# A new order and new PSUM homes for the first 552 steps of a retention and PReLU kernel on one core

## The chip, the cores and the metric

The kernel runs on one core of a Trainium2 chip. The metric is the device time of one execution in microseconds (us). A core has five engines that each work through their own queue in order: TensorE (PE; its weight loads are listed apart as PEld), VectorE (DVE), ScalarE (ACT), GpSimd (POOL), and SyncE (SP), which here issues nearly all DMA transfers. SBUF is the on-chip memory; PSUM holds matmul results in eight banks.

## The reference

```python
# q, k, v: (8, 8, 576, 64) float32
scores = scale * np.matmul(q, k.transpose(0, 1, 3, 2))
gamma = 1.0 - 2.0 ** (-5.0 - np.arange(H))
Dmat = np.where(rel >= 0, gamma[:, None, None] ** rel[None], 0.0)   # rel = i - j
attn = np.matmul(scores * Dmat, v)                                  # retention, per head
x = attn.transpose(0, 2, 1, 3).reshape(B * S, H * D)                # (4608, 512)
h = x @ w_in                                                        # w_in: (512, 2048)
g = np.maximum(h, 0.0) + alpha * np.minimum(h, 0.0)                 # alpha: (2048,)
out = g @ w_out                                                     # w_out: (2048, 512)
```

Both weights come as 64-bit floats; the kernel makes 32-bit ones of them on the chip.

## The kernel before, in words

**Retention.** A sequence of 576 positions is cut into nine chunks of 64. Within a chunk the masked product of q and k is formed; from chunk to chunk a running state (the sums of k times v, decayed) is carried. The first two batches are done in six "parts" of four, four and one chunks (all heads at once); the other batches later in pairs of heads ("joints"). For a part, SP loads the natural rows of k, q and v (`load_part`, into rooms of the tiles called w, so that the profile says `w<-in_k_dram`), GpSimd scales q and v by tables of powers of gamma (L351), TensorE transposes k and q (L375; L535 for the one-chunk part) and ScalarE copies the transposes out (L381, L538). Then come the products of q and k (L399) and VectorE's mask (L406), the states k times v (L422) with VectorE's sums (L435, L437), and the output, first from the masked scores (L470), then from the states (L493). Between L470 and L493 ScalarE makes a copy of one element (L482, "spy") that L493 waits for. ScalarE copies the result to the x tiles (L514). The one-chunk part has L548, L561 and L568 for these products.

A joint loads q and k in a form that VectorE can transpose (qx, kx; L722 in all), scales qx on GpSimd (L716), scales a natural k on ScalarE (kn, at L725 to L727), and forms scores and states on TensorE (L796, L803, L806), then the masks (L824), the carried sums (su, L836 to L847), and two copies by DMA into the tiles that the next joint's values product reads (L744): qT into `at`, su into `vn`.

**Weights.** A quarter of a weight unit is loaded as 64-bit words and turned into 32-bit floats by a chain: ScalarE (L613, L615), VectorE (L623, L625, L634), GpSimd (L637). After the first eight cells (see below), weights and activations are split into three parts each, so that fast 32-bit rounded matmuls add up to full precision: ScalarE L666, GpSimd L668 and VectorE L670 for weights, and the like for x and g.

**The MLP.** Tokens go in 18 blocks of 256, hidden columns in eight units of 256. The first eight (block, unit) cells use plain 32-bit matmuls, since their split weights don't exist yet: L974 for `x @ w_in`, ScalarE L980 and VectorE L985 for the PReLU, L1005 for the second product. All later cells use the split form (L1071, L1105 and L1223, L1167 at the end). While these run, the joints of the later batches are woven in between.

**Fills.** At the start there are matmuls whose result nobody reads: `burn` (L1297, 64 by 64 tiles with 16 columns, six groups of eight) and `fill` (L1288, 128 by 128, 15 in all). They are steps like others and have places in the order.

**What sets the order.** The kernel does not emit instructions as it is written. Every step is recorded by `do(engine, cost, function, reads, writes)`; 3811 steps are recorded. At the end the list ORDER, written out as numbers of steps, is gone through from its start, and each step then emits its instructions. So ORDER sets the order of every engine's queue, SP's among them; semaphores follow from the reads and writes. In the same way, each time a step needs a new PSUM tile, `Gen` takes the next digit of the string BANKS as its bank:

```python
if slot and slot.bank:
    slot = banks[int(next(banked))]
...
for now[0], n in enumerate(order):
    op = ops[n]
    ins = op.fn()
```

SP's loads are held back, too: for the first LIMITED entries of ORDER, `dma` makes a load wait for an earlier one's landing, so that no more than 1 MB (up to entry 130) or 1.25 MB is in flight:

```python
if now[0] < LIMITED:
    ahead = size
    for other, n in reversed(flight):
        if eng == "SP" and ahead >= (IN_FLIGHT if now[0] >= FRONT else IN_FRONT):
            tc.add_manual_dep(...)      # wait until `other` has landed
            break
        ahead += n
```

All loads by SP are recorded at L224 in the profile.

Of the kernel before, what the change touches and what calls it, by code (L numbers as in the profile page):

```python
# [21 lines left out]
def kernel(  # L22
# [126 lines left out]
    for i in range(2):  # L149
# [6 lines left out]
        "200535545661702405070423172047436234654317545707176141645461704500066171106600717116602607"  # L156
        "060167247052344635472107161067706117062653241061707601706104253461761006176107255234700761"
# [80 lines left out]
    LIMITED, IN_FLIGHT = 486, 5 << 18  # L238
# [1316 lines left out]
    for i, (va, vb) in enumerate(two):  # L1555
# [30 lines left out]
        "68-70 67 3 71 1-2 0 4-5 53 24 66 12 25 86 9 13-14 33 16 10 15 22 7 17 80 23 19 8 85 32 47 18 21 20 "  # L1586
        "27 48-50 84 6 115 83 51 26 64 55 52 28-29 56-57 87 81 118 58 119 88 30 59 62 82 63 40 114 116 65 60 "
        "154 112 34 31 54 117 110 113 11 72 111 36-37 139 61 136 138 140 38 142 35 153 141 137 171 41 43-44 "
        "89 39 42 168 143 94 166 144 95 103 73 145 90 45 146 46 155 147 181 156-157 209 182 75 170 183 76-77 "
        "102 158 74 159 91 93 160 92 212 161 184 162-163 204 78 121-122 97 176 185 129 96 98 177 99 104 100 "  # L1590
        "173 205 124 106 164 105 120 208 169 337 101 188-189 130 107-109 213 123 132 172 196 125-126 148 210 "
        "149 127 167 133 150 246 197 131 211 229 206-207 152 134-135 330 230 151 190 192-194 217 216 218 178 "
        "180 186 247 179 257 219 244 198 128 270 220 250 221 331 199 245 187 332 175 191 200 271 201-202 174 "
        "222 454 223 234-235 203 224-227 333 195 284-285 231 236 293 259 336 272 456 237 451 238-239 232-233 "
        "292 228 274 258 453 455 248 275 273 260-261 252 262 251 445 276 243 253 452 249 214 254 242 255 240 "
        "263 241 277 286 349 447 266 288 268 289-290 267 269 215 372 256 294 296-298 287 291 303 302 306 342 "
        "374 304 295 305 282 466 307 281 338 334 299 278 436 279 264 350 265 280 446 340 343 315 352-353 339 "
        "335 345 354 351 448 439 316 344 346 358 365 317 553 384 347 355 348 320 366 321 318-319 373 308 475 "
        "322 375 341 433 309 437 385 301 399 435 442 552 300 377 398 310-312 323-324 328 313 378 434 325 443 "
        "283 379 383 327 329 314 367 369 368 440 438 356 450 382 457 376 460 381 326 397 441 380 462 404 461 "  # L1600
        "79 415 414 360 467 413 361 405-410 402 458 411 400 412 417 419 359 362 416 363 423 422 421 165 364 "
        "403 401 444 392 463 393 386 459 387 468 357 465 481 555 482 420 424 449 388 418 394 426 464 396 425 "
        "472 490 370 473 395 522 488 519 523 483 520 526 489 495 529 487 507 469 496 389 497-498 390 499 524 "
        "501 505 427 506 478 504 517 500 503 539 493 485 568 371 502 428 492 484 521 530 527 476 528 534-535 "
        "540 532 541 516 508 533 430 391 542 491 536 543 537 544 494 545 470 538 582 486 514 474 480 581 509 "
        "583 477 510 512 511 513 515 431 471 618 595 584 531 588 570 590 596 546 597-599 569 586 563 548 585 "
        "594 547 593 571 549 564 607 587 479 601 604 600 561 589 616 562 565 620 572 566-567 573-575 606 554 "
        "592 634 603 619 605 636 602 577 591 432 635 617 614 551 608 576 615 610 550 637 578 621 638-639 "
        "622-623 640 651 609 612 655 624 652 429 648 641 653 611 613 658-661 654 662 674 579 643 665-668 656 "
        "697 647 669 663 670 695 671 696 664 688 672-673 690 675 689 580 677 687 657 649 642 644 698 645 650 "  # L1610
        "699-701 691-694 686 721 684 676 702 704 720 679 678 722 685 730 518 723 703 758 705 734-735 680-681 "
        "646 726 683 729 682 711 761 727 762 733 717 706 759 728 724 746 763 707-708 716 736 712 781 731 737 "
        "744 754 772 760 738-740 783 713-714 756 718 709 774-775 784 743 732 741 755 742 782 556 773 745 747 "
        "785-786 525 751 719 779 776 787 710 752-753 777 725 780 748 778 840 749-750 715 794-796 793 807 841 "
        "805 802 789 788 790 798 797 842 803 808-809 800 817 791 804 833 799 810 834 811-812 814 831 813 816 "
        "820 832 843 806 819 815 852 818 801 835 854 828-829 853 830 792 855-856 918 915 557 838 821 827 857 "
        "916 824 836 858 822 837 877 859 823 919 880 826 878 861 920 879 860 885 887 881 891 886 892-893 825 "
        "894 839 895 889 901 864 897 873 896 869 900 899 888 862 868 870-871 898 917 903 883 902 875 863 930 "
        "932 884 931 882 874 890 923 933 558-559 912 921 934 865-866 924 904 935 914 922 910 928 913 936 905 "
        "907 925 943 911 872 944 906 908 945-946 926-927 999 955 952 929 967 957 953 966 958-959 956 909 937 "  # L1620
        "954 876 948 960-962 939 942 969 949 951 991 1002 938 940 947 979 950 963 965 1004 968 998 1000 1003 "
        "1005-1007 992 964 867 757 971 989-990 993 1008 994 997 978 560 970 976 995 941 1028 625 1027 974 "
        "1029 1038 1001 977 1009 973 1010 975 1011 1050 1037 1041 1030 1068 1012 996 1065 1013 1042 1069 1014 "
        "1066 1015 1018 1067 1019 1051 1016 1071 1036 1035 972 1043-1044 1072 1020 1070 1073 1053 1034 1045 "
        "1047 1024 1046 1089 1033 1074-1075 1040 1049 1091 1048 1090 1063 1076 1052 1021 1079 1077 1092 1032 "
        "1055 1093 1039 1094 1060 1054 1064 1061 1095 1023 1017 1025-1026 1062 1031 1078 1059 1102 1056 1103 "
        "1111 1105 1104 1112 1141 1097 1110 1116 1106 1096 1098 1115 1099 1107 1100 1058 1113 1125 1148 1139 "
        "1057 1127 1117-1120 1122 1109 1121 1142 1114 1140 1126 1154 1150 1128 1152 1108 1153 1155 1143-1145 "
        "1124 1123 626 1101 1156 1129 1157 1371 1130 1022 1158 1147 1137 1159 1179 1136 1160-1161 628 1138 "
        "1177 1218 1178 1187 1162 1146 1163 1180 1149 1132 1219 1135 1133 1215 1220 1165 1201 1188 1164 1190 "  # L1630
        "1238 1131 1134 1185 1191 1216-1217 1192-1194 1239 1195 1197 1196 1203 1200 1173 1168 1175 1186 1240 "
        "1183 1231 1198 1166 1202 1170 1212 1184 627 1169 1151 1211 1174 1241-1242 1205 1232 1229 1204 1176 "
        "1199 1230 1171 1237 1243 1233 1181 1236 1244 1214 1208 1234 1206 1182 1235 1245-1246 1189 1210 1207 "
        "629-630 1253 1265-1266 631 1267 1252 1268-1269 1251 1261 1271 1247 1209 1213 1254 1249 1275 1288 "
        "1264 1289 1255 1298 1263 1270 1248 1274 1260 1262 1259 1277 1290-1292 1276 1295 1258 1257 1273 1279 "
        "632 1285-1286 1272 1293-1294 1278 1167 1287 1311 1297 1299 1172 1309-1310 1250 1312 1256 1313 1372 "
        "1314 1282 1315 1281 1336 1375-1376 1316 1284 1318 1335 1317 1334 1346 1348 1280 1349 1338 1357 1319 "
        "1350 1296 1331 1326 1345 1351 1330 1325 1283 1320 1373 1344 1352-1353 1342 1322 1446 1337 1377 1327 "
        "1341 1321 1374 1354 1358 1343 1328 633 1387 1355 1360 1378 1388 1379 1356 1389 1359 1340 1362 764 "
        "1369 1332 1300 1347 1339 1361 1390 1370 1323 1364 1391 1380 1366 1381-1382 1392-1393 1363 1383 1401 "  # L1640
        "1400 1402 1333 1413 1384 1447 1365 1367-1368 1404 1324 1411 1405 1412 1409-1410 1386 1459 1456 "
        "1414-1415 1455 1416-1417 1408 1407 1385 1423 1425 765 1418 1420 1419 1457 1424 1421 1403 1395 1406 "
        "1394 1460 1396 1422 1426 766 1427 1397 1461-1463 1436 1448 1521-1522 1449 1398 1430 1399 1434 1523 "
        "1453 1464 1450 1465 1485 1428 1524 767 1329 1435 768 1432-1433 1431 1484 1492 1451-1452 1466 1468 "
        "1467 1469 1491 1486 1498-1499 1493 1500 1454 1476 1501-1503 1429 1487 769 1508 1525 1480 1507 1528 "
        "1526 1489 1527 1496 1470 1495 1472 1490 1481 1504 1494 1471 1473 1546 770 1475 1547 1477 1505-1506 "
# [161 lines left out]
```

## Time and profile before

| | us |
|---|---|
| median of 3 runs | 915.4 (915.34 to 915.81) |
| profiled execution, its own time | 915.47 |
| its span in the profile | 913.4 |
| TensorE busy in it | 906.3 |
| granted TensorE clock (share of full) | 0.999 |

The profile is one execution on the core. "Busy" is the time in which an engine has an instruction running; matmuls are pipelined and their ends are modelled, so that short waits of TensorE can hide in busy time. A wait is put down to the engine or DMA that released it last. The view of waits gives total us, times and the longest; the timeline gives start, duration, engine, line, operation, output and inputs, with the idle time before it in brackets; the windows give busy us of each engine in a stretch, the clock, the mean busy share of the 16 DMA engines (which can read slightly over 1) and GB/s.

### The profile page before, as it was taken

How to read it: one execution, taken by the hardware profiler on the slowest of the kernel's cores; microseconds unless marked ns; L12 is line 12 of the kernel's file. 1: busy time of each engine (PE TensorE's matmuls, PEld its weight loads, DVE VectorE, ACT ScalarE, POOL GpSimd, SP SyncE). 2: the span in 40 equal slices, each digit the busy share in tenths (PEclk: the TensorE clock that was granted, in tenths of full speed). 3: DMA queues.
4: the chain of work that ended last, by engine and by line, in shares of the span. 5: the costliest groups of instructions: out<-in, count | busy, mean ns of one | idle time of the engine just before them, and what ended most of it. 6: DMA issues, size and time to landing. Idle time of an engine off the chain costs nothing. (4 is left out here: it accounts for less than half of the span.)

```text
span 913.4 us, 19163 instructions
## 1 busy us (share of the span) xinstructions
PE 906.3 (99%) x7331; PEld 739.6 (81%) x7331; DVE 549.6 (60%) x1004; ACT 500.7 (55%) x1011; POOL 520.3 (57%) x461
## 2 busy tenths in 40 slices
PE   9999999999999999999999999999999999999998
PEld 8767788887788888888888888888888888888886
DVE  5797767757768776576756776434444534444243
ACT  4575665556555665666746565636363636364441
POOL 4587665556556665756542335666655657574624
PEclk9999999999999999999999999999999999999999
DMA  9999778788898888775243332212122222211112
GB/s 204 245 232 185 172 173 184 166 204 186 185 200 192 205 208 189 177 182 167 70 141 130 99 115 82 70 58 81 57 93 64 91 82 76 93 47 47 46 47 70
DMA packets 235948, 121.34 MB, mean 133 GB/s; under 512 B 203456, under 2 KB 203728, under 8 KB 235856
## 3 DMA queue, kind: packets, MB, share of 16 engines
q1 hardware_dynamic: 235712, 119.98, 52.3%
q8 instruction: 58, 0.95, 0.5%
q14 instruction: 34, 0.28, 0.1%
q10 hardware_dynamic: 144, 0.13, 0.0%
HBM read 74.19 MB, written 32.51 MB: 117 GB/s over the span
## 5 line engine op out<-in xcount | busy, mean ns | idle before, releaser
L1223 PE MATMUL pso<-w,g 128*128 128x512 f32 x1344 | 330.3, 392 | 0.0
L1223 PEld LDWEIGHTS pso<-w,g 128*128 128x128 f32 x1344 | 249.9, 188 | 54.3 <-POOL g L1150 1.6
L1147 POOL TENSOR_TENSOR g<-ga_all,g 128x512 fp32r<-128x512 f32 x76 | 98.2, 1295 | 131.5 <-ACT g L1143 101.8
L1150 POOL TENSOR_TENSOR g<-g 128x512 fp32r<-128x512 f32 x114 | 147.3, 1295 | 19.4 <-DVE su L949 5.7
L1071 PE MATMUL psa<-lx_x,w 128*128 128x512 f32 (+1 forms) x288 | 70.3, 377 | 0.2 <-DVE at L824 0.2
L1071 PE MATMUL psh<-lx_x,w 128*128 128x512 f32 (+1 forms) x272 | 68.2, 384 | 0.1
L1143 ACT ACTIVATE g<-ga_all 128x512 fp32r<-128x512 f32 x76 | 47.8, 631 | 36.6 <-PE pso L1223 17.5
L1139 POOL TENSOR_TENSOR g<-g 128x512 fp32r<-128x512 f32 x22 | 28.5, 1297 | 61.8 <-DVE g L1136 34.4
L1071 PEld LDWEIGHTS psa<-lx_x,w 128*128 128x128 f32 x288 | 51.4, 188 | 12.1 <-issue 1.3
L1071 PEld LDWEIGHTS psh<-lx_x,w 128*128 128x128 f32 x272 | 49.6, 188 | 11.2 <-issue 0.6
L1223 PE MATMUL pso<-lx_x,g 128*128 128x512 f32 x216 | 53.5, 390 | 0.1
L1147 POOL TENSOR_TENSOR g<-vn,g 128x512 fp32r<-128x512 f32 x25 | 32.4, 1297 | 37.2 <-ACT g L1143 34.5
L1145 ACT ACTIVATE g<-ga_all 128x512 fp32r<-128x512 f32 x76 | 47.2, 624 | 5.8 <-PE pso L1223 4.0
L1046 POOL TENSOR_TENSOR lx_x<-lx_x 128x512 fp32r<-128x512 f32 x28 | 35.9, 1293 | 23.1 <-DVE lx_x L1043 18.9
L1223 PEld LDWEIGHTS pso<-lx_x,g 128*128 128x128 f32 x216 | 40.4, 188 | 9.0 <-DVE o L1246 0.6
L1241 DVE TENSOR_TENSOR op<-pso,op 128x512 f32<-128x512 f32 x35 | 24.0, 686 | 31.2 <-PE pso L1223 31.2
L1071 PE MATMUL pso<-lx_x,w 128*128 128x512 f32 (+1 forms) x160 | 37.8, 370 | 0.0
L1105 PE MATMUL psh<-w,w 128*128 128x512 f32 x144 | 34.6, 389 | 0.0
L1105 PE MATMUL psa<-w,w 128*128 128x512 f32 x144 | 34.6, 389 | 0.0
L716 POOL TENSOR_TENSOR qx<-qx,tabx 128x576 f32<-128x576 f32 x24 | 27.6, 1149 | 9.6 <-DMA qx<-in_q_dram 5.9
L1071 PEld LDWEIGHTS pso<-lx_x,w 128*128 128x128 f32 x160 | 28.0, 188 | 5.7 <-ACT o L1245 0.6
L1147 POOL TENSOR_TENSOR g<-x,g 128x512 fp32r<-128x512 f32 x13 | 16.9, 1298 | 26.2 <-ACT g L1143 24.7
(408 smaller groups left out, 1968.2 us busy)
## 6 DMA issues: line engine op xcount, KB each, us to landing
xk<-x SPq DMA_DIRECT2D x18, 512.0 KB, 3.7
ok<-o SPq DMA_DIRECT2D x36, 256.0 KB, 2.7
op<-ok SPq DMA_DIRECT2D x18, 512.0 KB, 4.0
out_dram<-o SPq DMA_DIRECT2D x35, 256.0 KB, 2.3
x<-xk SPq DMA_DIRECT2D x16, 512.0 KB, 5.5
kx<-in_k_dram SPq DMA_DIRECT2D x96, 72.0 KB, 3.3
qx<-in_q_dram SPq DMA_DIRECT2D x96, 72.0 KB, 3.3
kn<-in_k_dram SPq DMA_DIRECT2D x48, 144.0 KB, 3.6
```

What stands on the lines that cost most here:

```text
L716: return nc.gpsimd.tensor_tensor(out=qh, in0=qh, in1=tabx[:, None, c, :, None].to_broadcast([P, NJ, 2, 32]), op=ALU.mult)
L1046: do("POOL", 1.29, lambda h=h, l=l, d=d: nc.gpsimd.tensor_tensor(out=piece(d()), in0=h(), in1=l(), op=ALU.subtract), [(g, 0, n), (g, 1, n) ...
L1071: nc.tensor.matmul(out_of(p), w[:, c0:c0 + P], xp(l, cc), start=(l != 1 and cc == 0), stop=(l > 0 and cc == NCC - 1))
L1105: nc.tensor.matmul(p.get(), w[:, c0:c0 + P], piece(words_of(g)[:, o:o + DM]), start=(l != 1 and cc == 0), stop=(l > 0 and cc == NCC - 1))
L1139: do("POOL", 1.29, lambda: nc.gpsimd.tensor_tensor(out=piece(to.get()[:, 2]), in0=to.get()[:, 0], in1=to.get()[:, 1], op=ALU.subtract), [( ...
L1143: do("ACT", 0.64, lambda: nc.scalar.mul(piece(to.get()[:, 2]), whole(), BELOW), both, [(to, 2)])
L1145: do("ACT", 0.64, lambda: nc.scalar.mul(piece(to.get()[:, 0]), whole(), BELOW * 2.0 ** -12), both, [(to, 0)])
L1147: do("POOL", 1.29, lambda: nc.gpsimd.tensor_tensor(out=piece(to.get()[:, 1]), in0=whole(), in1=to.get()[:, 2], op=ALU.subtract), both + [( ...
L1150: do("POOL", 1.29, lambda: nc.gpsimd.tensor_tensor(out=piece(to.get()[:, 2]), in0=to.get()[:, 0], in1=to.get()[:, 1], op=ALU.subtract), [( ...
L1223: nc.tensor.matmul(a[2 * m + b].get(), piece(g.get()[:, l, f, m * P:(m + 1) * P]), w_piece(u, 2 + f, l), start=(cell["first"] and f == 0 a ...
L1241: do("DVE", 0.69, lambda: nc.vector.tensor_tensor(out=t(), in0=p1.get(), in1=t(), op=ALU.subtract), [(p1, 0)], [tk])
```

## The change

The first 552 entries of ORDER are rearranged; they are the same steps. From entry 552 on the list is unchanged. Of the first 111 digits of BANKS 77 differ, and LIMITED goes from 486 to 492. The new list and digits were found by a search in which every instruction fetch has a random time. Nothing else differs. The diff, cut to its start:

```diff
     BANKS = (
-        "200535545661702405070423172047436234654317545707176141645461704500066171106600717116602607"
-        "060167247052344635472107161067706117062653241061707601706104253461761006176107255234700761"
+        "440236123203724560764414054717561230515671214535401603745574765057165171016600717616062006"
+        "701760203652344625743107161067706117062653241061707601706104253461761006176107255234700761"
 ...
-    LIMITED, IN_FLIGHT = 486, 5 << 18
+    LIMITED, IN_FLIGHT = 492, 5 << 18
 ...
     ORDER = (
-        "68-70 67 3 71 1-2 0 4-5 53 24 66 12 25 86 9 13-14 33 16 10 15 22 7 17 80 23 19 8 85 32 47 18 21 20 "
-        "27 48-50 84 6 115 83 51 26 64 55 52 28-29 56-57 87 81 118 58 119 88 30 59 62 82 63 40 114 116 65 60 "
+        "66-67 2 68 71 3 13 1 0 4-5 69 80 53 70 9-10 85 16 12 24 17 14 25 22 83 15 7 23 86 19 8 47 18 21 84 "
+        "48 27 49 20 81 50-51 82 6 114 116 87 32 115 26 55 117 56 52 33 110 88 57-60 72 136 118-119 65 112 64 "
 ...
```

Some of the queues before and after (fill and L-numbers as above, step numbers in brackets):

```text
SP, first 21 loads (k, q, v: attention; wi, wo: w_in, w_out; al: alpha)
 before: k q q k v v | wi wi q wi al q wi k k v v wo q wo k
 after:  q k q k v v | al q wi wi k q k v wi wi v wo q wo k
PE, after the first part's states (L422)
 before: fill fill L470 L470 al L375 L493 L493 fill L375 fill L375 L375 fill L399 L399 L422 L974 L422 L974 L535
 after:  al fill L375 L470 L470 L375 L493 L493 L375 fill L375 fill fill fill L399 L399 L422 L422 L974 L974 L535
ACT, at entry 360 or so
 before: L666(475) spy(322) kn(375) L666(433) L666(442) L514 ...
 after:  L615(344) L666(433) kn(375) spy(322) L514 L514 L514 L514 ...
SP, second half of the first joint's kn (step 339)
 before: entry 332, ahead of both loads into op
 after:  entry 357, behind loads of qx, kx, both loads into op and the copy of qT into at
```

## The prediction

> **What bounds the kernel now.** I read the busy times first, then the windows, then every wait of TensorE, and last the queues around the waits in the part that the change touches.
>
> ```profile
> PE 906.3 (99%) x7331; PEld 739.6 (81%) x7331; DVE 549.6 (60%) x1004; ACT 500.7 (55%) x1011; POOL 520.3 (57%) x461
> ```
>
> TensorE is the bound: it is idle for 913.4 - 906.3 = 7.1 us. The windows (PE, PEld, DVE, ACT, POOL busy, clock, DMA share, GB/s) say where:
>
> ```profile
> 0.00:30.00 30.00, 27.57 (x609) 24.82 (x613) 20.07 (x66) 12.59 (x21) 16.08 (x29) 1.00 0.99 212
> 30.00:70.00 40.00, 40.00 (x580) 28.89 (x573) 32.13 (x56) 26.90 (x51) 27.34 (x25) 1.00 0.96 238
> 70.00:115.00 45.00, 44.67 (x678) 32.98 (x677) 35.49 (x73) 25.37 (x58) 31.59 (x28) 1.00 0.88 177
> 115.00:900.00 785.00, 784.53 (x5438) 645.38 (x5437) 457.14 (x804) 435.24 (x881) 442.67 (x380) 1.00 0.47 123
> ```
>
> The first 30 us lose 2.4, the next 85 us 0.3, the 785 us after that 0.5, and the rest is the tail. Up to 70 us the DMA engines are as full as TensorE (share 0.99 and 0.96): two bounds run side by side. The whole run's waits of TensorE (us in total, times, longest):
>
> ```profile
> PE psh L1297 <- DVE warm L101: 1.1, 1, 1.1
> PE psa L535 <- DMA w<-in_k_dram: 0.4, 1, 0.4
> PE pso L422 <- POOL w L351: 0.4, 1, 0.4
> PE psa L470 <- ACT ga_all L980: 0.3, 1, 0.3
> PE psa L375 <- DMA w<-in_k_dram: 0.2, 1, 0.2
> PE pso L1167 <- POOL g L1139: 0.2, 1, 0.2
> PE psa L1071 <- DVE at L824: 0.2, 1, 0.2
> ```
>
> All but the sixth lie ahead of 103 us, which is the stretch that is reordered. The first is the start itself.
>
> **What the change moves.** The first 552 entries of ORDER hold the same 552 steps in both kernels, and from there on the two lists are equal: by the order view that stretch ends on TensorE about 113 us in. No step is added or dropped, also not the fills and burns (L1288, L1297), which cost TensorE the same wherever they stand. So the sum has only waits in it, and switches between small and full tiles. It is made against the profiled execution: span 913.4, time 915.47, that is 2.1 outside the span and 0.07 above the median of 915.4.
>
> *Early waits.* Open to a gain ahead of 30 us: 0.4 + 0.4 + 0.2 = 1.0, and some 0.5 that the modelled ends hide (L1288 ends at 20.44 + 0.83 = 21.27, L399 starts at 21.43; others are like it). There is one alternation less: before, small L422 stands between two L974 groups, 25.50 - 23.57 = 1.93 apart, where unbroken L974 takes 41.35 - 39.63 = 1.72 for as many: 0.2. Ceiling 1.7. But then comes the wait on the load:
>
> ```profile
> 28.48 0.71 PE L535 MATMUL psa<-ident,w 64*128 64x64 f32 x8 [0.37 <-DMA w<-in_k_dram]
> ```
>
> That k load is the 21st on SP's queue in both orders, behind the same 20 loads, in a window with a DMA share of 0.99. Whatever TensorE saves ahead of it is waited away, unless the queue itself runs faster. Also, the second L422 group now stands directly behind the first, and needs GpSimd's second scaling of v:
>
> ```profile
> 21.85 2.04 POOL L351 TENSOR_TENSOR w<-w,tp 128x512 f32<-128x512 f32 x2 [2.16 <-DMA w<-in_v_dram]
> ```
>
> It ends at 23.9, and its load again has the same set ahead of it, so a new wait of about 1 us stands there, paid for out of what was saved before. From 23.9: L422 0.5, two L974 groups 3.5, switches 0.4, gives 28.3, just ahead of 28.48. Bounds for the early part: 1.7 gained to 1.0 lost; I take 0.1 gained, by the k load's row.
>
> *Middle waits.* L470's 0.3 and L1071's 0.2 can go (vector steps of L985 come sooner, another PSUM bank is written). Bounds 0 and 0.5; I take 0.3.
>
> *One dangerous place, at 80 us.* ScalarE's one-element copy L482 ("spy") releases L493, and before it stands ahead of the scaling of kn (the profile calls it L727):
>
> ```profile
> 76.53 0.13 ACT L482 COPY spy<-psh 1x2 f32<-1x2 f32 x1
> 76.57 0.77 ACT L727 ACTIVATE kn<-kn,tabk 128x576 f32<-128x576 f32 x1
> 80.32 0.27 PE L493 MATMUL psa<-w,w 64*64 64x64 f32 x2
> ```
>
> After it, L727 stands first and the spy right behind. L727 needs both halves of kn, and the second half has moved far back on SP: behind more qx and kx loads, both weight halves into op and the copy of qT. Behind the waiting L727 are queued on ScalarE the spy and four L514 copies; behind L493 on TensorE, everything. L493 is due at about 80.9 (L548, 0.56, goes ahead of it now). From kn's landing it needs 0.1 + 0.77 + 0.15 + 0.1 = 1.1, so kn must land by 79.8. When does it? Counting bytes along SP's list, the load of before with as many ahead of it is issued here:
>
> ```profile
> 76.82 0.46 SPq L224 DMA_DIRECT2D qx<-in_q_dram  x1
> ```
>
> With 4.0 to 5.2 to landing (the DMA issues from 60 to 100 us: kn 4.0, op 5.2) kn lands at 80.8 to 82.0 and L493 waits 1.0 to 2.2. Against it stands that in before SP itself stood still ahead of a weight load, held by the bound on bytes in flight:
>
> ```profile
> SPq L224 <- DMA kx<-in_k_dram: 3.3, 2, 3.2
> ```
>
> With fewer loads ahead of that weight load, up to 3.2 of this may come back, and kn lands at 77.6, with no wait. Bounds 0 and 2.2; with the DMA engines at 0.96 most of the 3.2 was not idle time, so I take 80.6, that is 0.8 lost.
>
> *Edits at no cost.* LIMITED's rise from 486 to 492 by itself reaches no load: SP's entries around it stand at 481 and 496 of the new order. PSUM homes cost nothing by themselves: a new home is a new wait on its last reader, and I found none later than those above. The su copies into vn (L224) leave about 3 us later, since six more vector steps (L722 twice, L824 four times, 3.5 us by their rows) now stand ahead of L847; the second was issued at about 88.6 and landed 2.8 later, at 91.4, and L744 reads it at 95.53, so about 1 us of cover is left; if it is gone, L744 waits by as much as it is short.
>
> Sum: 915.4 - 0.1 - 0.3 + 0.8 = 915.8.
>
> **A rule that speaks against the change.** Of the instruction fetch the page's part on DMA queues shows (packets, MB, share):
>
> ```profile
> q8 instruction: 58, 0.95, 0.5%
> ```
>
> No row of TensorE's waits names it, so here a fetch can only act through the DMA engines that it shares with loads. The Trainium skill, "Runtime: NRT & Kernel Launch", section "Instruction fetch mechanics", says that the fetch runs ahead by itself and is mostly hidden. By that rule there is nothing random to plan for, and the time would be 915.4. The trace agrees as far as TensorE's waits go; what a fetch does to a load's landing no view shows.
>
> **Rivals.**
>
> 1. *Robust front, faster.* SP's queue really runs ahead (k and v of the second part arrive sooner since two w_in loads stand behind them, the 3.2 us hold is gone), so that the early 1.7 and the middle 0.5 both come back and kn is in time: 915.4 - 2.2 = 913.2. For it: the waits are there to be had. Against it: equal sets of loads ahead of both early gates at a share of 0.99.
> 2. *The spy waits, slower.* kn lands at its late bound, 82.0, nothing later gives it back, since TensorE runs without gaps from 81 us on, and the early part loses a little: 915.4 + 2.2 - 0.3 + 0.4 = 917.7, up to 918.5 when the su copies are short as well. It decides at kn's landing: 79.8 costs nothing, and from there each us costs one; it is slower by over 0.2% beyond about 82.
> 3. *Nothing happens*, because every gain runs into the DMA queue and kn is just in time: 915.4. It lies inside the forecast's case.
>
> **How the numbers follow.** A measurement of this kernel can tell about 0.2%, 1.8 us, from no change. Forecast and rival 3 together 0.48, with a range of their own of 914.2 to 917.0; rival 1 0.17; rival 2 0.35, more than rival 1 since a gain needs several waits to go at once and a loss only one. Faster by over 0.2% (under 913.6) is rival 1, slower (over 917.2) is rival 2. The range reaches into both, to 913.2 and 918.3, and leaves out about a tenth on each side at most.
>
> **What would show it.** In the profile of the changed kernel: L535 near 28.5 still released by a DMA, or the early part was misjudged; a wait of the second L422 on POOL L351 near 23; L470 and L1071 gone from TensorE's waits; L493 near 81 with a wait on ACT L482, and ScalarE's L727 ahead of it released by kn's DMA. If L727 starts before 79.9, the 0.8 is wrong; if TensorE idles by over 1 us anywhere from 30 to 115 us at another line, so is the picture. Past 115 us every line should cost what it costs now.

## The result and the profile after

The changed kernel takes 919.74 us (median of 6, 918.91 to 921.28) beside 915.5 for the kernel before: ratio 1.005, 95% interval 1.004 to 1.0061. It is slower by 4.2 us. In three later sets of executions, each with the kernel before beside it, the same kernel stood at 1.0028 (1.0018 to 1.0038), 1.0043 (1.0031 to 1.0056) and 1.0038 (1.0025 to 1.0052): always slower, by 2.3 to 4.2 us. Why its four medians lie 2.2 us apart (917.55 to 919.74), and those of the kernel before only 0.5 (915.0 to 915.5), is part of the story. The profiled execution took 919.4 us, span 917.7.

The windows of the changed kernel (columns as before):

```profile
0.00:30.00 30.00, 26.33 (x546) 24.12 (x546) 18.35 (x64) 11.79 (x20) 14.41 (x27) 1.00 0.96 204
30.00:70.00 40.00, 39.55 (x627) 29.20 (x627) 31.19 (x55) 28.09 (x53) 27.43 (x25) 1.00 0.96 241
70.00:115.00 45.00, 43.21 (x655) 30.25 (x655) 34.75 (x67) 23.31 (x50) 28.27 (x25) 1.00 0.76 164
115.00:900.00 785.00, 784.52 (x5449) 645.96 (x5447) 457.52 (x808) 436.98 (x887) 444.73 (x382) 1.00 0.48 123
```

TensorE's idle time grows in all three early stretches: from 2.43 to 3.67, from 0 to 0.45 and from 0.33 to 1.79 us. In the last line TensorE's busy time is the same to 0.01. TensorE's waits say which ones they are (us in total, times, longest):

```profile
PE pso L535 <- DMA w<-in_k_dram: 1.6, 1, 1.6
PE psa L493 <- ACT spy L482: 1.4, 1, 1.4
PE psa L1297 <- DVE warm L101: 1.1, 1, 1.1
PE psa L422 <- POOL w L351: 0.8, 1, 0.8
PE psh L974 <- DVE su L847: 0.3, 1, 0.3
PE pso L1005 <- DVE lx_w L634: 0.3, 1, 0.3
PE psa L1071 <- DVE at L824: 0.2, 1, 0.2
```

L535's wait has grown from 0.4 to 1.6. L493's for the spy is new, so are those of L974 and L1005. L470's is gone. The timeline at the two large ones:

```profile
29.84 0.68 PE L535 MATMUL pso<-ident,w 64*128 64x64 f32 x8 [1.59 <-DMA w<-in_k_dram]
...
83.65 0.78 ACT L727 ACTIVATE kn<-kn,tabk 128x576 f32<-128x576 f32 x1 [4.73 <-DMA kn<-in_k_dram]
84.33 0.13 ACT L482 COPY spy<-psh 1x2 f32<-1x2 f32 x1
84.52 0.27 PE L493 MATMUL psa<-w,w 64*64 64x64 f32 x2 [1.44 <-ACT spy L482]
```

ScalarE stands 4.73 us in front of the kn scaling with the spy queued behind it, and TensorE stands behind the spy. kn landed at 83.63, not at 80.6.

Where the 4.2 us arise can be read from TensorE's progress: L535 starts 1.36 later than before (29.84 against 28.48), the first L1005 1.3 later (33.98 against 32.67), the second L535 group 2.3 later (75.95 against 73.65) and the first L744 4.2 later (99.76 against 95.53). At each of the last three points TensorE has done as many products in both kernels (703, 1191 and 1527). Up to L744 its idle time has grown by 3.2 us, from 2.73 to 5.91; the other 1.0 stands in no row of waits. From that L744 to the end of the span it is 817.9 us in both kernels, and 817.8 to 818.6 in all 17 profiles of this study. So the time is settled by 100 us, and a run is read by when it reaches L744:

| kernel | ratio to before (95%) | L535 | kn landed | L493 | L744 |
|---|---|---|---|---|---|
| before | 1 | 28.5 | 75.8 | 80.3 | 95.5 |
| changed, first profile | 1.0050 (1.0040 to 1.0061) | 29.8 | 83.6 | 84.5 | 99.8 |
| c_after | 1.0028 (1.0018 to 1.0038) | 28.8 | 81.7 | 82.6 | 97.9 |
| c2_after | 1.0043 (1.0031 to 1.0056) | 28.8 | 83.5 | 84.4 | 99.6 |
| c3_after | 1.0038 (1.0025 to 1.0052) | 30.4 | 84.0 | 84.9 | 100.2 |
| e1_spy_first | 1.0025 (1.0012 to 1.0039) | 28.5 | 82.8 | 81.9 | 97.2 |
| e2_k_ahead | 1.0035 (1.0023 to 1.0047) | 27.5 | 81.7 | 82.6 | 97.8 |
| e3_su_first | 1.0029 (1.0013 to 1.0045) | 28.6 | 82.1 | 83.0 | 97.7 |
| e4_burn_homes | 1.0040 (1.0027 to 1.0053) | 28.2 | 81.0 | 81.9 | 97.2 |
| e5_three | 1.0006 (0.9998 to 1.0015) | 28.6 | 80.5 | 80.6 | 95.4 |
| e7_no_spy | 1.0030 (1.0019 to 1.0042) | 29.8 | 82.7 | 83.6 | 98.3 |
| g1_both_waits | 1.0019 (1.0010 to 1.0028) | 27.3 | 81.1 | 81.3 | 96.1 |
| k1_load_early | 1.0018 (1.0010 to 1.0027) | 28.6 | 77.0 | 81.4 | 96.6 |
| e6_half_burns | 1.0049 (1.0036 to 1.0062) | 30.3 | 85.6 | 86.4 | 101.7 |
| f1_before_late | 1.0038 (1.0025 to 1.0051) | 28.4 | 82.0 | 82.9 | 99.7 |
| f3_load_only | 1.0008 (0.9999 to 1.0017) | 27.7 | 80.4 | 79.2 | 95.1 |
| h1_k_ahead | 1.0005 (0.9996 to 1.0014) | 28.0 | 75.4 | 80.0 | 95.2 |

The times of a column are those of one profile each; the ratio is over all executions of a set. The runs were made in four later sets, each with the kernel before beside it and each on another chip: e1 to e4; c_after, e5, e6 and f1; c2_after, e7, g1 and f3; c3_after, k1 and h1. From one set to another, ratios are compared.

### The profile page after: what moved, and what is told of

Its sections match the earlier page's. It is cut to its first block, busy times and chain, and to the rows that moved or that the text cites. A ratio compares the mean times of both kernels' runs of the same rounds, so it can differ in the third digit from the quotient of the medians.

```text
span 917.7 us, 19153 instructions
## 1 busy us (share of the span) xinstructions
PE 907.3 (99%) x7331; PEld 740.1 (81%) x7331; DVE 549.8 (60%) x1004; ACT 501.9 (55%) x1011; POOL 520.0 (57%) x461
## 5 line engine op out<-in xcount | busy, mean ns | idle before, releaser
L1071 PE MATMUL psa<-lx_x,w 128*128 128x512 f32 (+1 forms) x284 | 69.2, 376 | 0.2 <-DVE at L824 0.2
L1071 PE MATMUL psh<-lx_x,w 128*128 128x512 f32 (+1 forms) x272 | 68.5, 385 | 0.1
L1139 POOL TENSOR_TENSOR g<-g 128x512 fp32r<-128x512 f32 x22 | 28.5, 1295 | 61.8 <-DVE g L1136 34.4
L1071 PEld LDWEIGHTS psa<-lx_x,w 128*128 128x128 f32 x284 | 50.8, 188 | 11.5 <-issue 0.8
L1071 PEld LDWEIGHTS psh<-lx_x,w 128*128 128x128 f32 x272 | 49.6, 188 | 11.7 <-issue 1.1
L1071 PE MATMUL pso<-lx_x,w 128*128 128x512 f32 (+1 forms) x164 | 38.6, 370 | 0.1
L1071 PEld LDWEIGHTS pso<-lx_x,w 128*128 128x128 f32 x164 | 28.5, 188 | 6.5 <-ACT o L1245 0.6
L824 DVE SCALAR_TENSOR_TENSOR at<-psa,pf,mask 64x512 f32<-64x512 f32 (+1 forms) x46 | 24.0, 526 | 14.4 <-PE psa L803 6.9
L716 POOL TENSOR_TENSOR qx<-qx,tabx 128x576 f32<-128x576 f32 x24 | 27.7, 1154 | 7.3 <-DMA qx<-in_q_dram 6.0
```

Of the source, the lines that this page charges most:

```text
L716: return nc.gpsimd.tensor_tensor(out=qh, in0=qh, in1=tabx[:, None, c, :, None].to_broadcast([P, NJ, 2, 32]), op=ALU.mult)
L824: nc.vector.scalar_tensor_tensor(out=mt.get()[half(1 - h2), h2, j], in0=fro[x], scalar=pf[x, 1, h:h + 1], in1=mask[x, None, :].to_broadcas ...
L1071: nc.tensor.matmul(out_of(p), w[:, c0:c0 + P], xp(l, cc), start=(l != 1 and cc == 0), stop=(l > 0 and cc == NCC - 1))
L1139: do("POOL", 1.29, lambda: nc.gpsimd.tensor_tensor(out=piece(to.get()[:, 2]), in0=to.get()[:, 0], in1=to.get()[:, 1], op=ALU.subtract), [( ...
```

## The experiments

All edits are moves in ORDER, written as the list of step numbers, unless it says otherwise.

**The spy behind kn.** Theory: kn's second half lands late, and through the spy this holds up TensorE. Rivals: the value part L493 is late for its own inputs, or the delay is covered later. First the changed kernel with the two ScalarE steps in the old order (e1_spy_first):

```diff
-375 322 383
+322 375 383
```

> The changed kernel with one step moved: the spy copy (L482, step 322) is issued ahead of the kn scaling (L727, step 375) on ScalarE; all else stays. Theory A (kn's late landing reaches TensorE only through the queue place of the spy): the 1.4 us wait of L493 for the spy goes, L493 starts at about 83.0 instead of 84.5 us, everything behind it is 1.2 to 1.5 us earlier, and the kernel takes about 918.3 us. kn is landed at 83.6, scaled by 84.4, and its first reader (the score products L796) comes at 86.1 to 86.3, so no new wait. Rival B (the value part is late for another reason, its own inputs or its PSUM homes): L493 starts at 84.4 or later as before and the time stays at 919.7. Rival C (the score products inherit the wait for kn): less than 0.5 us comes back. Since the steps up to 80 us are the same ones, the places of the instruction packets on the DMA engines (one at 79.7 us in the changed kernel) should be seen again within 0.3 us if they follow TensorE's instruction count; if they are random, kn lands at another time.

kn landed late again, at 82.8, and TensorE did not care. ScalarE's timeline in this run:

```profile
77.90 0.13 ACT L482 COPY spy<-psh 1x2 f32<-1x2 f32 x1
82.81 0.78 ACT L727 ACTIVATE kn<-kn,tabk 128x576 f32<-128x576 f32 x1 [4.77 <-DMA kn<-in_k_dram]
```

The spy is done 4.8 us before kn is there, L493 has no wait, and it starts at 81.9. That is theory A in the profile. The instruction packet expected at 79.7 came at 78.95, with TensorE 0.9 us ahead of the changed kernel's first profile (the second L535 group at 75.05 against 75.95). In time the run (1.0025) can't be told from the unchanged kernel's 1.0028 to 1.0050, so the price needed stronger contrasts. One is the kernel before with the pair alone made late (f1_before_late), and with the load late but the spy in front (f3_load_only):

```diff
 f1, in the kernel before
-339 ... 322 375 ... 377 ... 323
+377 339 375 322 ... 323
 f3, in the kernel before
-339 ... 322 375 ... 377 ... 323
+322 ... 377 339 375 ... 323
```

> The kernel before with one part of the change alone: SyncE's kn load (339) is issued behind the qx load (377), four places later than its place before, and the spy copy (322) and the kn scaling (375) on ScalarE go behind it in the changed kernel's order (scaling first). Theory A (this pair is the largest single cause): kn lands at 82.3 to 83.5 us instead of 75.8, L727 and the spy end 0.9 us later, L493 starts at 83.4 to 84.4 us instead of 80.3, and nothing later makes up for it: 3.0 to 4.0 us slower than the kernel before, about 918.7. Rival B (the late value part is covered by what follows, since the changed kernel loses its time elsewhere): less than 1 us slower. Rival C (the load lands early although it is issued late, for lack of a fetch packet in its way): kn lands at 81.0, 1.5 to 2.2 us slower.

> f1_before_late without its second half: in the kernel before, the kn load (339) and its scaling (375) go four places later, but the spy copy (322) keeps its place ahead of the scaling. Theory A (the late kn reaches TensorE through the spy, and without that only through what ScalarE has queued behind the scaling): L493 starts at 80.1 to 80.5 us as in the kernel before, the copies L514 behind the scaling are 1.5 to 2.0 us late, the score products L796 start at 84.3 to 85.5 instead of 83.8, and the time is 0.5 to 1.7 us above the kernel before, 915.8 to 917.0. Rival B (the score products inherit the whole of it): 3.0 us or more above, as f1_before_late's 3.4.

TensorE's longest wait in f1:

```profile
PE psa L493 <- ACT spy L482: 2.9, 1, 2.9
```

f1 is 3.4 us slower than the kernel before (918.69 against 915.29), as expected; kn landed at 82.0 and L493 started at 82.9, both a little under their ranges. Not all of it is the wait. The windows of f1 around the wait (columns as before):

```profile
79.93:83.34 3.41, 0.50 (x25) 0.40 (x28) 0.00 (x0) 0.81 (x2) 1.91 (x3) 1.00 1.19 153
83.34:86.76 3.42, 3.42 (x71) 2.79 (x63) 1.23 (x3) 1.99 (x5) 0.00 (x0) 0.50 0.75 166
```

TensorE was busy for 0.50 of 3.41 us and was then granted half its clock for the next 3.42; from L493 to L744 it took 16.77 us, against 15.20 in the kernel before. Four of f1's five executions have a mean granted clock of 0.998 or less (this profile: 0.997), and none of f3's eleven has.

f3, with kn landing 4.6 us later than in the kernel before, stands at 1.0008, and its interval holds no change. L493 has no wait there, but the L514 copies queued behind the scaling now hold up another step:

```profile
PE psh L974 <- ACT x L514: 0.6, 1, 0.6
```

By the ratios, 0.0030 of 915, or 2.7 us, hang on the queue place of a one-element copy, the half clock included; the two intervals together allow 1.3 to 4.2. L493 (79.2) and L796 (82.7) started earlier in f3 than expected because L535's load landed early in that profile, at 27.45.

The other contrast moves the load instead and leaves the spy behind (k1_load_early, beside c3_after):

```diff
-553 398 552 377 339 (on SyncE)
+339 553 398 552 377
```

> The changed kernel with kn's load (step 339) issued on SyncE ahead of the 256 KB load 553 (at about 75 us) instead of four issues later behind the qx load 377 (77.5 us); ScalarE keeps the scaling ahead of the spy. Theory A (kn is late first for its place in SyncE's queue, and its last sixteenth for the instruction packet that is fetched at about 79 us, which at the earlier place is behind it): kn's fifteenth part lands at 77.6 to 78.8 us and its sixteenth within 0.5 us of it, L727 starts as soon as ScalarE is free at 78.9, the spy ends by 80.0, L493 does not wait, and the time is 0.8 to 2.2 us below the unchanged changed kernel. Rival B (the place of the spy is what counts, not the load's): L493 still waits over 0.5 us and the time is that of the changed kernel. Rival C (what is issued behind kn is now late instead: the qx load 377 or the load 552): a new wait of over 0.5 us at L796 or L1005 and less than 0.5 us gained.

```profile
77.35 0.76 ACT L727 ACTIVATE kn<-kn,tabk 128x576 f32<-128x576 f32 x1
78.02 0.13 ACT L482 COPY spy<-psh 1x2 f32<-1x2 f32 x1
...
81.35 0.27 PE L493 MATMUL psa<-w,w 64*64 64x64 f32 x1
```

kn is there at 77.0, and no row waits for kn or for the spy. The run is 1.7 us faster than the unchanged kernel beside it (916.93 against 918.66), though the intervals of the two ratios just overlap. Four issues on SyncE and one place on ScalarE are two ways to cure the same wait.

**The other waits.** The state recurrence in one piece (e3_su_first), and a PSUM home of its own for each group of burns, of which three in a row had one (e4_burn_homes):

```diff
 e3
-417 405 360 406 416 ... 407 ... 408 ... 409 ... 410
+405 406-410 417 360 416
 e4, BANKS
-764414
+764513
```

> The changed kernel with the state recurrence of the first half on VectorE in one piece, as before the change: steps 405, 407 to 410 (L838, L844, L847) go directly ahead of the transposes and masks (L722, L829, L832) instead of between them; the ScalarE copy 406 goes with them. Theory A (the second L974 at 93.8 us waits 0.3 to 0.4 us because the recurrence holds its PSUM home until L847 ends at 94.3): the wait goes, L847 ends by about 92.3, time 0.4 us shorter, 919.3. Rival B: the masks and transposes that are now later hold up the next products (L744, at 99.8), and nothing comes back, 919.7 or more.

> The changed kernel with two digits of the PSUM homes changed: of the six groups of warm-up products (steps 66 to 71) three in a row share pso2 in the changed kernel; here each has a home of its own. Theory A (what is won ahead of L535 is lost again at its load, since SyncE's first loads are paced by landings and not by TensorE): the two stalls of 0.28 us at 3.6 and 4.7 us go, the first transposes start at 6.6 instead of 6.88 us, L535 still starts at 29.7 to 29.9, and the time stays at 919.7 within 0.15. Rival B: the 0.33 us is carried to the end, 919.4.

In e3 the wait of L974 for L847 is gone from TensorE's waits, and L744 has no wait; by the profile theory A holds. In e4 the first transposes start at 6.37 instead of 6.87, and L535 at 28.2, earlier than expected but right behind its load, which landed at 28.07. Neither ratio differs from the unchanged kernel's, so both are undecided as to the time. Next, all four edits together, the fourth being VectorE's rounding chain, which L1005 waits for, ahead of a step that waits for GpSimd (e5_three), and the same without the spy's edit (e7_no_spy):

```diff
 e5: e1, e3, e4 and
-447 282 446 253-255
+282 446 253-255 447
 e7: e5 with
-322 375
+375 322
```

> The changed kernel with four of its steps put right at once: the spy copy (322) ahead of the kn scaling (375), the state recurrence (405 to 410) in one piece, a PSUM home of its own for each burn, and the wait of L1005 at 65.7 us for the rounding chain (DVE steps 253 to 255, L623 to L634) taken away by issuing the L670 step 447, which waits 0.6 us for GpSimd, behind that chain instead of ahead of it. Theory A (the loss is these waits and the spread of L535's load): L493's 1.4 us, L974's 0.35 us and L1005's 0.3 to 0.5 us go, so 2.2 to 2.6 us less than the changed kernel, that is 0.2 to 0.9 us above the kernel before: 915.4 to 916.1 if the kernel before is at 915.2. Rival B (a price that every line past 115 us pays for the new order): the waits go and it stays over 917.0.

> e5_three without its first edit: the spy copy stays behind the kn scaling, as in the changed kernel; the recurrence, the rounding chain and the burns' homes stay mended. Theory A (the spy's place alone costs 0.9 to 1.4 us): L493 waits 0.8 to 1.6 us for the spy again and the time lies 0.9 to 1.4 us above e5_three, at 1.0016 to 1.0021 of the kernel before. Rival B (the wait only takes slack that TensorE spends elsewhere in e5_three): within 0.4 us of e5_three, 1.0006 to 1.0010. Against the unchanged changed kernel beside it, theory A expects 0.8 to 1.2 us less, from L974's 0.35 and L1005's 0.55.

All of TensorE's waits in e5:

```profile
PE pso L535 <- DMA w<-in_k_dram: 1.3, 1, 1.3
PE psa L1297 <- DVE warm L101: 1.1, 1, 1.1
PE pso L422 <- POOL w L351: 0.8, 1, 0.8
PE psa L1071 <- DVE at L824: 0.4, 2, 0.2
PE psa L422 <- POOL w L351: 0.4, 1, 0.4
```

The spy, L974 and L1005 are gone, L744 starts at 95.4, and the time is 915.6, level with the kernel before (1.0006, no change inside the interval) and 0.0022, or 2.0 us, below the changed kernel beside it (c_after, 1.0028), with the intervals apart. So nothing past 100 us costs more in the new order: rival B falls. e7, in another set, is at 1.003: by the ratios the spy's place is worth 0.0024 of 915, that is 2.2 us. The two intervals together allow 0.8 to 3.6, so this can't be told from the 0.9 to 1.4 expected. In the two profiles 1.1 us arise where the spy stands (from the second L535 group to L493: 7.92 against 6.83), and most of the other 1.9 by which e7 reaches L744 later is already there at L535 (1.25). The three edits that e7 keeps give 0.5 us by the medians (917.86 against 918.39 for c2_after beside it) and 1.2 by the ratios, less than the intervals can tell.

**The early wait.** The k load that L535 waits for, ahead of the 512 KB load (e2_k_ahead); with e5 and the ScalarE copy that L548 needs moved too (g1_both_waits); and in the kernel before (h1_k_ahead, meant to beat both kernels):

```diff
 e2
-138 40 153 35 155
+138 153 40 35 155
 g1: e5, e2 and
-41 74 181-182
+181-182 41 74
 h1, in the kernel before
-72 ... 153
+153 72
```

> The changed kernel with one SyncE load moved: the second part's last k load (step 153, 128 KB) is issued ahead of the 512 KB weight load (step 40) instead of behind it; all else stays. Theory A (L535's 1.6 us wait is the place of its load behind a 512 KB load whose last sixteenth was held up by instruction packets at 23.6 and 24.4 us): the k load lands at 25.5 to 27.5 instead of 29.7, L535 starts as soon as the L974 group ahead of it lets it, at 28.1 to 28.4 instead of 29.85, and the lead of about 1.4 us stays up to 75 us; kernel about 918.4. Rival B (the wait moves to the next step that needs one of the held-up loads, the weights of step 40 at L1005 at 34 us): L535 early, but L1005 starts at 34.0 as before and the time stays at 919.7. Rival C: the gain is eaten later by the kn load, which lands by SyncE's queue at 83.6 whatever TensorE does: the wait at L493 grows from 1.4 to 2.6 and the time stays at 919.7; partly so would give 919.0 to 919.5.

> e5_three with its remaining early wait taken away too: SyncE issues the k load (153) ahead of the 512 KB weight load (40), as in e2_k_ahead, and on ScalarE the copy that L548 needs (L538, step 182) goes ahead of the L613 step (41) that waits for that weight load, so that it is no longer queued behind it. Theory A (in e2_k_ahead the 1.4 us moved from L535 to L548 only because of this queue place): L535 starts at 27.3 to 28.0 us, L548 waits 0.3 us or less, the first L1005 starts at 32.2 to 32.9 us (32.67 in the kernel before), and the time is 0.5 to 1.2 us below e5_three: 914.4 to 915.3, level with the kernel before or up to 0.8 us below it. Rival B (the weight load itself is the limit, through the rounding chain that L1005 needs): L1005 starts at 33.2 or later and the time is that of e5_three, 915.6.

> An attempt at a version faster than both: the kernel before with the k load that L535 waits for (step 153, 128 KB) issued ahead of the 512 KB load 72 instead of behind it, nothing else. Theory A: the k load lands at 25.5 to 27.0 us instead of 28.4, the wait of 0.4 us at L535 goes, L535 starts at 28.0 to 28.1, and the time is 0.2 to 0.4 us below the kernel before. Rival B (as in e2_k_ahead and g1_both_waits, TensorE then waits for the next of the early loads, at L548, L493 or L1005): L1005 starts at 32.6 us or later, as in the kernel before, and the time is the same within 0.2 us or up to 0.5 us longer.

In e2 TensorE's timeline shows the wait pass from one line to another:

```profile
27.45 0.68 PE L535 MATMUL pso<-ident,w 64*128 64x64 f32 x8
30.73 0.68 PE L548 MATMUL pso<-w 64*64 64x64 f32 x16 [1.42 <-ACT w L538]
```

ScalarE had the copy for L548 queued behind a step that waits 2.8 us for the 512 KB load (wa L613). With that cured in g1, L535 starts at 27.3 and L548 has no wait, but the waits of the early part are now these:

```profile
PE pso L493 <- ACT spy L482: 0.8, 1, 0.8
PE pso L375 <- POOL w L351: 0.7, 1, 0.7
PE psh L375 <- POOL w L351: 0.5, 1, 0.5
```

L1005 starts at 33.45, later than in e5 (32.68), and the ratio is not below e5's (1.0019 against 1.0006). Both fit rival B, but that the weight load is the limit is not shown: GpSimd (L351) waits 1.1 us for q loads there, but the spy, at 30.14, stands behind three steps of ScalarE's own work (L613, L615, L980, from 28.53 on). Taking one wait away has shown the next. h1 gains nothing either (1.0005), though L535 starts 0.5 earlier. No version of this study beats the kernel before.

**Is it the instruction packet?** In the traces a load lands in 16 parts, as many as there are DMA engines. In the changed kernel 15 parts of the late kn load had landed at 81.65 and the last at 83.63; a 16 KB instruction packet had been fetched at 79.72 and took 1.15 us. I tried to move that packet by making TensorE's program shorter (e6_half_burns):

```diff
-        burn(8)
+        burn(4)
```

> The changed kernel with half of its warm-up products left out (six groups of 4 instead of 8; they compute nothing that is used). TensorE's instruction stream is 96 records shorter ahead of the first load, and the profile of the changed kernel has one 16 KB instruction packet for every 256 TensorE records, so each later packet should be fetched 96 records later. Theory A (kn's last sixteenth is held up by the packet that is fetched at 79.7 us, and packets follow TensorE's count): the packet moves from 79.7 to 82.5 or later, kn's sixteenth part lands within 0.8 us of its fifteenth, at 81.0 to 82.0 us, the wait of L493 for the spy falls to 0.5 us or less, time 0.9 us or more below the unchanged changed kernel's on the same chip, unless the shorter warm-up costs it back at the first transposes, which would show as a later L399 (10.5 us). Rival B (the sixteenth part is late for its place in SyncE's queue, or packets come at random): the gap between the fifteenth and the sixteenth part stays at 0.8 to 2.0 us and the wait at 0.8 to 1.6 us.

This settled nothing. L535's load landed at 30.18 and L535 waited 3.4 us, all later issues slid back with it, and the packet (82.35) and the kn load (issued at 80.47) kept nearly the same distance; the last part came 0.73 us behind the fifteenth. TensorE had half its clock from 29.44 to 36.27 there, and all six executions of e6 have a granted clock of 0.998 or less. The count was no good guide either: the packet came at TensorE's record 2588, the changed kernel's at 2684, which is 96 less, just as many as were left out; so it stayed with the same instruction and did not keep the same count. The time was no better for the shorter warm-up.

What stands for the packet is a comparison over the 17 profiles. Of 1398 transfers that SyncE issued, that landed from 5 to 100 us and whose parts are all on record, 266 had their fifteenth part land 0.5 to 2 us after the end of a 16 KB packet: their last part came 0.75 us later in the mean, and over 0.6 us later in 65% of them. For the 188 with 8 us or more since a packet it was 0.22 us, and 9%. The late kn load alone shows the same: in the ten profiles in which a packet ended 0.8 to 2.0 us ahead of its fifteenth part, the last came 0.66 to 1.98 us behind it, and in the four in which that packet ended 2.9 us or more ahead (c_after, e5, f1, f3), 0.21 to 0.61. That is a strong relation, not an experiment: a kernel in which only the packet moves was not found.

**The unchanged kernel again** (c_after, c2_after, c3_after):

> The changed kernel once more, unchanged, beside the kernel before on the same chip, to see what of its profile is the same from run to run. Theory A (the places of the instruction packets follow TensorE's instruction count, but what a packet holds up varies): L493 waits for the spy by 0.8 to 1.6 us again, kn's last sixteenth lands 0.8 to 2.0 us after its fifteenth again, while the wait of L535 for its k load lies anywhere between 0.4 and 1.6 us; time between 918.2 and 919.7 beside 915.2 before, so 3.0 to 4.3 us slower. Rival B (all of it is fixed by the order): the same waits within 0.2 us and 919.7.

> The changed kernel once more, unchanged, as the measure for the other kernels of this set, since it stood 4.2 us above the kernel before in its first set of executions and 2.3 us in the second. Theory A (the waits are the same in kind, their lengths vary with what an instruction packet holds up): 2.0 to 4.5 us above the kernel before; L493's wait for the spy between 0.8 and 1.6 us, L535's for its load between 0.4 and 1.6. Rival B (a property of the program alone): one of the two former values again with the same waits within 0.2 us.

> The changed kernel unchanged, as the measure for the next kernel on the same chip. Both theories: 2.3 to 4.3 us above the kernel before, with L493 waiting 0.8 to 1.6 us for the spy.

Neither the fixed waits of rival B nor the spreads expected: the spy's wait was 0.9, 1.3 and 0.3, L535's 1.0, 1.7 and 2.3, and c_after's 917.55 lies under its range. In c3 the spy waited less because TensorE was late already (the second L535 group at 77.51, against 75.95 in the first profile). And two of the three show something that no row of the waits has. Windows of c2_after around L535 (columns as before):

```profile
26.03:29.44 3.41, 1.71 (x15) 1.20 (x14) 3.36 (x7) 1.22 (x2) 1.03 (x2) 1.00 1.20 173
29.44:32.86 3.42, 3.42 (x116) 3.42 (x118) 1.43 (x4) 1.81 (x4) 2.18 (x3) 0.50 0.93 255
32.86:36.27 3.41, 3.41 (x53) 2.39 (x48) 1.48 (x5) 2.64 (x5) 1.91 (x3) 1.00 0.89 236
```

TensorE waited 1.70 us for the k load, was busy for 1.71 of 3.41 us, and was then granted half its clock for the next 3.41 us. L535 starts at 28.83 in c2 and at 28.82 in c_after, but L1005 at 34.39 against 32.97: 1.4 us for a wait that was already over. In e7 a longer wait, 2.26, lay across two such windows and had no such price:

```profile
25.10:28.51 3.41, 2.45 (x11) 1.65 (x10) 3.06 (x7) 0.84 (x2) 1.44 (x2) 1.00 1.04 188
28.51:31.93 3.42, 2.12 (x91) 2.08 (x91) 2.08 (x3) 2.07 (x6) 2.07 (x2) 1.00 0.76 192
```

## Why the prediction was wrong

The forecast was 915.8 and the range ended at 918.3. The spy's wait behind kn was in it with the right mechanism; the sizes of all three terms were wrong, two of them in sign, and one kind of wait, that on PSUM homes, was put at nothing. In the first profile the stretch up to the first L1005 lost 1.3 us (forecast: 0.1 gained), from there to the second L535 group 1.0 was lost (forecast: nothing), and from there to L744 1.9 (forecast: 0.8 lost, less up to 0.3 gained at L470).

- **"I take 80.6, that is 0.8 lost."** The right place, mis-sized. kn landed at 83.63, beyond the late bound of 82.0 too, and L493 waited 1.4. The step that failed is the bound: SyncE issued the load at 77.55 instead of 76.8, and it took 6.1 us to land, where I had taken the loads' medians (4.0 to 5.2) as the end of the range and then subtracted some of SyncE's 3.2 us hold. The hold for kx went, but SyncE stood for other things instead (from 60 to 85 us 2.1 us for GpSimd's L637 and 1.2 for a w_in load), and a median says nothing of the last sixteenth of one load: here it came 1.98 us behind the fifteenth. Over all profiles of the changed order with the load at that place that gap was between 0.2 and 2.0. The price of the place over all executions came out above the 1.4 of the first profile, at 2.2 us by e5 and e7 and 2.7 by f1 and f3, but with intervals that hold 1.4 as well.
- **"Whatever TensorE saves ahead of it is waited away"; 0.1 gained.** The gate was right, its date wrong. The load is the 21st in both orders, behind the same 20, the last of them a 512 KB load of w_out in both. SyncE issued it 0.22 us later (23.14 against 22.92), its fifteenth part landed 0.45 later (28.75 against 28.30), and its last part came 0.96 behind that instead of 0.14. So the k load landed at 29.71 instead of 28.44, and between 28.69 and 30.31 in the three repeats; L535 lost 1.36 instead of gaining 0.1. Why the last part came so late is open. The 512 KB load ahead of it had a gap of 0.99 here and of 0.05 in the kernel before, but here the last 16 KB packet had ended 2.7 us ahead of its fifteenth part and before only 0.6 us ahead, the reverse of the relation above. The second L422's wait for GpSimd was there as forecast (0.8 against about 1).
- **"L470's 0.3 and L1071's 0.2 can go"; 0.3.** Half right: L470's went, L1071's stayed at 0.2. But a stretch that the sum took as unchanged got longer: from the first L1005 to the second L535 group it is 41.0 us in all four profiles of the old order and 41.6 to 42.2 in the eleven of the changed one other than e5 and g1 (41.1 and 41.0). TensorE's idle time there shows 0.2 to 0.8 of this; e7, which has e5's edits but the spy's, is among the eleven, so what the rest is stays open.
- **"PSUM homes cost nothing by themselves ... I found none later than those above."** Wrong, with waits of about 1 us in all in the profiles: three groups of burns in one home (0.32 at the first transposes, 6.87 against 6.55, ahead of L535's wait for its load), L1005 on a home that the rounding chain still holds (0.3 of wait), L974 on the home that the recurrence holds until L847 (0.3). What they cost in time the runs can't tell (e3, e4, e7). The six vector steps that I had found ahead of L847 do hold something up; I priced them at the su copies, where the cover held (L744 has no wait), and not at the home.
- **"Past 115 us every line should cost what it costs now."** Right: 817.9 us from L744 to the end.
- **Rival 2** had the mechanism and 917.7. The sets came out at 917.6 to 919.7: it was the case that happened, with the early part's loss too small in it and nothing for the middle. What would have shown the picture wrong, over 1 us of idle time at another line, did not occur between 30 and 115 us: the one wait of that size there was the spy's.
- **The rule of the fetch.** I used the Trainium skill, "Runtime: NRT & Kernel Launch", section "Instruction fetch mechanics", by which a fetch is mostly hidden, for a rival without any change. TensorE's waits agree with it in 16 of 17 profiles. What speaks against taking it as "no effect" is the relation above: by it, the fetch would be hidden from TensorE and not from the loads that TensorE waits for, which no run here settles.

## What to carry to other kernels

A tiny step that releases the bounding engine should never be queued behind one that waits for a DMA: look at what stands ahead of it on its in-order engine. When a load is gated by its last sixteenth, price its landing by the spread of single loads, not by the median of a row. And where TensorE and the DMA engines are both full, don't count on a wait that is taken away: in this kernel's first 35 us L535's wait came up again at L548 (e2) and then at L375 and L493 (g1).

## What the runs showed of the hardware

- **A window that was half idle was enough for the clock to fall.** The changes of TensorE's granted clock lie on a grid of 3.41 us (stretches of 17.07, 20.48 and 904.53 us are 5, 6 and 265 of them). In 17 profiles, four windows of that grid ahead of the program's end had TensorE busy for 50% or less (0.15 in f1, 0.28 in e6, 0.32 in c3, 0.50 in c2), and each was followed by 3.41 us or more at half clock. No window of 0.55 or more (e3's 0.55, e2's 0.58, the changed kernel's 0.60) was, where the clock was full before. So a wait of 1.7 us can cost 1.4 us more (c2), and whether it does depends on where the grid lies. This is one reason why the same order spreads from run to run: of 24 executions of the changed kernel itself 7 have a mean granted clock of 0.998, and in their sets they are 1.3 to 2.0 us slower in the mean than the others; of 81 executions of the kernel before in the later sets 4 have 0.998 or less. The Trainium skill, "TensorE: Matmul & The Clock Gate", section "What's actually happening", states a free-running window of 3413 ns, with which the grid agrees; its rule to avoid idle gaps of over about 3.4 us (section "HAM oscillation — how this bites in real kernels") is too wide for this kernel: 1.70 us was enough.
- **TensorE idle with nothing to wait for.** In h1, and in no other profile, TensorE stood still in the middle of a row of small products:

```profile
18.06 0.27 PE L493 MATMUL psh<-g,w 64*64 64x64 f32 x2 [0.98 <-issue]
```

A 16 KB packet had been fetched at 15.68 (in the kernel before: at 13.45) and was done at 16.64; TensorE stopped at 17.08. So the stop began 0.4 us after that packet was in. That it has to do with the late fetch is a guess, which no run tests.
